# The global P V for both heads at once, dense pieces 0, 1, 2, 1 per step, and the local 1e-9 left on VectorE

## The chip, the core and the metric

The kernel runs on one core of a Trainium2 chip. The metric is the device time of one execution in microseconds; a program is compared by the median of several executions. The core has five engines with instruction streams of their own: TensorE (PE; its weight loads are listed as PEld), VectorE (DVE), ScalarE (ACT), GpSimd (POOL) and SyncE (SP, which issues most DMAs). They wait for each other by semaphores, and each engine runs its own stream in order.

## What is computed

Three layers follow each other. The first is attention with local and global tokens (batch 4, 8 heads, 512 local and 32 global tokens, head size 64, window 32); the second a dense layer of 512 → 2048 → 512 with PReLU on the 2176 tokens; the third sends each token to one of 8 experts. The change lies in the attention and in the part of the dense layer that runs beside it.

```python
def sm(s):
    s = s - np.max(s, axis=-1, keepdims=True)
    e = np.exp(s)
    return e / (np.sum(e, axis=-1, keepdims=True) + 1e-09)
s_g = scale * np.matmul(q_g, k_all.transpose(0, 1, 3, 2))      # 32 global rows see all 544 keys
out_g = np.matmul(sm(s_g), v_all)
s_ll = np.where(mask, scale * np.matmul(q_l, k_l.transpose(0, 1, 3, 2)), -1000000000.0)
s_lg = scale * np.matmul(q_l, k_g.transpose(0, 1, 3, 2))       # 512 local rows: window + 32 global keys
out_l = np.matmul(sm(np.concatenate([s_lg, s_ll], axis=-1)), np.concatenate([v_g, v_l], axis=2))
...
h = x @ w_in                                                   # the dense layer
g = np.maximum(h, 0.0) + alpha * np.minimum(h, 0.0)
x = g @ w_out
```

## The kernel before

**Units, pairs, steps.** A unit is one batch and two heads; there are 16 units, handled in 8 pairs p. A pair takes four steps j = 0 to 3 of 128 local positions (STEPS = 4), so that n = 4p + j runs from 0 to 31, with two more steps to drain. The order on TensorE, VectorE and ScalarE in the attention is the order of the program text (manual_schedule); on GpSimd and SyncE a scheduler sets it.

**One step** (attention, L489 to L536) is in this order: dense.turn (ScalarE: neg, the ReLU part of a finished dense product); norm of step n − 1 (VectorE L404, L405, L407: add 1e-9, reciprocal, scale the probabilities); scores of step n (TensorE s L391; VectorE L397 adds the mask and takes the maximum; ScalarE L399 exponentials with their sum); dense.close (VectorE g L559, ScalarE's ghi and GpSimd's glo, the high and low part of g for an exact product); two decoding operations on VectorE (fill "V": L85, L88, L90, L92, which unpack the dense layer's weights); the bank o and dummy products on it (L520); dense.products (six matmuls, L571 for the first dense product, L585 for the second); one of the four pieces of the global rows; more decoding; pv of step n − 2 (TensorE o L424, ScalarE's copy L426); ptrans of step n − 1 (TensorE t L413, ScalarE's copy L415); and ScalarE's decoding operations.

**The global rows.** Their pieces run at j = 1, 2, 3 and at j = 0 of the next pair: gscores (TensorE L440, VectorE L441, ScalarE exponentials L445), gnorm (VectorE L449 to L453: 1e-9, reciprocal, scaled probabilities into gpat), gtrans (six transposes gt L463, copies L464), gpv (go L473, copied into xb by L475). gpat is a fixed tile with zeros where no window has its own positions; GW names six windows that together cover all positions.

**The dense layer beside it.** From step 12 (BEG) a first chunk of 272 tokens (CH) goes through eight blocks f of the first product, twelve matmuls each in two halves of six, and from step 28 through the second product, block by block, into two accumulators (h) of the same pool h1. rest() does what is left of the second product behind the attention, and the GEMM stage (gemm, L208) follows; it decodes the other half of the weights, one part every ten yields. xl L73 and xh L72 are the low and high part of the next chunk's tokens xb.

**Banks.** PSUM tiles o and go rotate over the same pools: a new tile waits until the reader of the one that had its bank is done.

Of the kernel before, what the change touches and what calls it, by code (L numbers as in the profile page):

```python
# [25 lines left out]
def tile_attention_moe_moe(ctx: ExitStack, tc: tile.TileContext, qkw, vw,  # L26
# [285 lines left out]
    with ExitStack() as at:  # L312
# [115 lines left out]
        GW = (1, 4, 7, 10, 13, NQ - 2)  # L428

        def gscores(p, part):  # L430
            d = G[p]
            if part == 0:
                d["s"] = (gp.tile([128, NG], F32, name="gsc"), gp.tile([128, 4], F32, name="gmx", bufs=2))
            sc, mx = d["s"]
            lo, hi = (0, S) if part == 0 else (S, NG)
            s = bank([128, hi - lo], f"gs{part}")
            for i in range(2):
                k = U[2 * p + i]["k"]
                x = k[:, WIN:2 * WIN] if part else k[:, 2 * WIN:KL - WIN].rearrange("p (m c) -> p m c", c=3 * WIN)[:, :, :2 * WIN]
                T.matmul(s[64 * i:64 * i + 64], U[2 * p + i]["g"], x, start=True, stop=True)  # L440
            V.tensor_tensor_reduce(out=sc[:, lo:hi], in0=s, in1=gzero.to_broadcast([128, hi - lo]), scale=-D ** -0.5,  # L441
                                   scalar=mx[:, 0:1] if part else BIG, op0=OP.add, op1=OP.min,
                                   accum_out=mx[:, part:part + 1])
            if part:
                A.activation(out=sc, in_=sc, func=AF.Exp, bias=mx[:, 1:2], scale=-1.0, accum_out=mx[:, 2:3])  # L445

        def gnorm(p):
            sc, mx = G[p]["s"]
            V.tensor_scalar(mx[:, 2:3], mx[:, 2:3], 1e-9, None, op0=OP.add)  # L449
            V.reciprocal(mx[:, 3:4], mx[:, 2:3])  # L450
            own = gpat[:, 2 * WIN:KL - WIN].rearrange("p (m c) -> p m c", c=3 * WIN)[:, :, :2 * WIN]
            V.tensor_scalar(own, sc[:, :S].rearrange("p (m c) -> p m c", c=2 * WIN), mx[:, 3:4], None, op0=OP.mult)
            V.tensor_scalar(gpat[:, 4 * WIN:5 * WIN], sc[:, S:], mx[:, 3:4], None, op0=OP.mult)  # L453

        def gtrans(p, part):
# [5 lines left out]
            for i in range(n):  # L461
                o = kpos(GW[4 * part + i])
                T.transpose(t[:, i], gpat[:, o:o + KW], ident)  # L463
            (V.tensor_copy if part else A.copy)(d["t"][:, 4 * part:4 * part + n], t)  # L464

        def gpv(p):
            d = G[p]
            o = bank([128, 2, SG], "go")
            for i in range(2):
                for n, w in enumerate(GW):  # L470
                    r = slice(96 if w == NQ - 2 else 0, 128)
# [14 lines left out]

        def pieces(p):
            return [(0.8, lambda: (gscores(p, 0), gscores(p, 1))), (0.0, lambda: gnorm(p)),
                    (0.6, lambda: (gtrans(p, 0), gtrans(p, 1))), (1.2, lambda: gpv(p))]  # L489

        def attention():
# [9 lines left out]
            for n in range(N + 2):  # L501
# [9 lines left out]
                if n < N:  # L511
                    scores(p, j)
                dense.close(n)
# [24 lines left out]
        class dense:  # L538
            ps, ys, g = None, [], None

            def turn(n):
                f = (n - BEG) // 2 - 1
                if 0 <= f < KH and (n - BEG) % 2 == 0:
                    dense.neg = gh_.tile([128, CH], F32, name="neg")
                    A.activation(out=dense.neg, in_=dense.ps, func=AF.Relu, scale=-1.0)

            def close(n):
# [8 lines left out]
                f = (n - BEG) // 2 - 1  # L556
                if 0 <= f < KH and (n - BEG) % 2 == 0:
                    g = gh_.tile([128, CH], F32, name="g")
                    epi[0] = V.scalar_tensor_tensor(g, dense.neg, al1[:, f:f + 1], dense.ps, op0=OP.mult, op1=OP.add)  # L559
                    split(dense.g[0][:, f], dense.g[1][:, f], g, lo_eng=P)  # L560

            def products(n):
                f, half = divmod(n - BEG, 2)
                if f < 0:
                    return
                if f < KH:
                    if not half:
                        dense.ps = pH.tile([128, CH], F32, name="h1", tag="h1")
                    for k in (0, 1) if not half else range(2, KD):
# [3 lines left out]
                    return  # L573
                f = n - BEG - 2 * KH
                if not f:
                    dense.ys = [pH.tile([128, CH], F32, name="h1", tag="h1") for _ in range(2)]
                for d in range(2):
                    for _ in dense.second(d, (f,)):
                        pass
                dense.done = f + 1  # L580
# [9 lines left out]
            def rest():  # L590
                dense.ys += [pY.tile([128, CH], F32, name="y", tag="y") for _ in range(2)]
                most = KH - 2
                for d, fs in ((2, range(most)), (3, range(most))) + tuple(
                        (d, range(dense.done if d < 2 else most, KH)) for d in range(KD)):
                    yield from dense.second(d, fs)
                    if fs[-1] == KH - 1:
                        xd = gx.tile([128, CH], F32, name="xd", bufs=2)
                        A.copy(xd, dense.ys[d])
                        nc.sync.dma_start(out=xpart[d, :, :CH], in_=xd)
# [44 lines left out]
        gpat = mk.tile([128, KL], F32, name="gpat")  # L644
# [857 lines left out]
```

## Time and profile before

| | before |
|---|---|
| median of 3 runs | 819.95 us (819.55 to 821.95) |
| the profiled execution | 818.03 us |
| its span in the trace | 816.3 us |
| mean granted TensorE clock | 0.992 |
| TensorE busy, share of the span | 782.0 us, 96% |
| VectorE busy | 457.5 us, 56% |
| ScalarE busy | 392.6 us, 48% |
| GpSimd busy | 355.8 us, 44% |

A busy time says how long an engine worked, not whether its work set the end. Three other views tell that: the busy time of all engines in one stretch, the list of what each engine waited for, and the chain of waits, which goes back from the last instruction, at each step to what released it. In a timeline the figure in brackets at a row's end is the idle time of the engine ahead of that row, and what ended it.

### The profile page before, as it was taken

The numbers are of one execution on the slowest core, as the hardware profiler recorded it, in microseconds if no ns is written. First come the engines' busy times: TensorE is split into PE (matmuls) and PEld (weight loads), VectorE is DVE, ScalarE is ACT, GpSimd is POOL, SyncE is SP. The second block draws the span as 40 slices with busy tenths as digits, with TensorE's granted clock in tenths as the row PEclk, the third lists the DMA queues.
The fourth block names the chain that finished last, engine by engine and source line by source line (L and its number), as shares of the span: only waits on it lengthen the run. The fifth ranks groups of instructions, "written<-read, shape, count | busy, mean of one in ns | idle before, by whom it ended". The sixth has DMA issues, their size and how long they took to land.

```text
span 816.3 us, 20877 instructions
## 1 busy us (share of the span) xinstructions
PE 782.0 (96%) x8298; PEld 728.1 (89%) x8298; DVE 457.5 (56%) x1587; ACT 392.6 (48%) x983; POOL 355.8 (44%) x308
## 2 busy tenths in 40 slices
PE   6989897998999999999999999999999999999996
PEld 4767776898999999999999999999999999989994
DVE  5889997445556531434343357777767778652210
ACT  5777876444445533333333434342455655444431
POOL 1122222033445343300000555663799988688611
PEclk9999997999999999999999999999999999999999
DMA  9988785153433122022221216424376666566510
GB/s 341 374 300 284 284 301 169 52 173 125 133 126 91 50 84 83 7 65 69 74 92 56 83 55 214 128 66 156 101 226 200 204 212 182 155 186 207 189 55 28
DMA packets 53851, 121.98 MB, mean 149 GB/s; under 512 B 4600, under 2 KB 26040, under 8 KB 51705
## 3 DMA queue, kind: packets, MB, share of 16 engines
q1 hardware_dynamic: 50825, 111.73, 42.1%
q0 software_dynamic: 2928, 8.92, 3.0%
q8 instruction: 65, 1.06, 0.5%
q14 instruction: 33, 0.27, 0.1%
HBM read 102.80 MB, written 17.83 MB: 148 GB/s over the span
## 4 chain that ended last, share of the span: by engine, by line
PE 77%; DVE 9%; issue 5%; DMA 5%; POOL 2%; ACT 2%; SPq 0%; POOLq 0%; DVEq 0%; ACTq 0%
PE h L200 21%; PE h L1258 10%; PE h L1122 10%; PE y L239 9%; PE h L1102 8%; PE o L424 3%; PE s L391 2%; PE go L473 2%; DMA raw<-in_moe_w_in_dram 2%; PE h L1335 2%; PE lp L282 2%; PE t L413 1%; DMA raw<-in_moe_w_dram 1%; PE pc L938 1%; DVE sc L397 1%
## 5 line engine op out<-in xcount | busy, mean ns | idle before, releaser
L73 POOL TENSOR_TENSOR m<-raw,m 128x1024 fp32r<-128x1024 f32 x64 | 152.2, 2398 | 15.8 <-ACT m L72 12.8
L200 PE MATMUL h<-xh,win 128*128 128x272 f32 x704 | 138.5, 291 | 2.1 <-ACT xd L245 2.1
L200 PEld LDWEIGHTS h<-xh,win 128*128 128x128 f32 x704 | 111.9, 188 | 4.6 <-ACT xd L245 2.3
L73 POOL TENSOR_TENSOR gr<-gb,gr 128x272 fp32r<-128x272 f32 x64 | 48.0, 776 | 149.3 <-ACT gr L72 148.9
L1102 PE MATMUL h<-xsh,m 128*128 128x272 f32 x512 | 103.3, 293 | 0.0
L200 PE MATMUL h<-xl,win 128*128 128x272 f32 x352 | 101.3, 288 | 0.0
L1258 PE MATMUL h<-gr,wout 128*128 128x272 f32 x672 | 95.1, 294 | 0.0
L73 POOL TENSOR_TENSOR glo<-g,ghi 128x272 fp32r<-128x272 f32 x64 | 54.5, 856 | 91.2 <-ACT ghi L72 79.8
L1122 PE MATMUL h<-hh,m 128*128 128x272 f32 x448 | 91.4, 295 | 0.0
L1258 PEld LDWEIGHTS h<-gr,wout 128*128 128x128 f32 x672 | 87.0, 189 | 0.4 <-ACT gr L72 0.4
L239 PE MATMUL y<-ghi,wout 128*128 128x272 f32 x448 | 86.9, 290 | 0.0
L72 ACT CAST m<-raw 128x1024 fp32r<-128x1024 f32 x64 | 66.0, 1049 | 39.6 <-DMA raw<-in_moe_w_dram 39.6
L205 ACT ACTIVATE neg<-h 128x272 f32<-128x272 f32 x120 | 47.6, 397 | 71.2 <-PE h L200 70.5
L1102 PEld LDWEIGHTS h<-xsh,m 128*128 128x128 f32 x512 | 81.7, 189 | 0.1
L1102 PE MATMUL h<-xsl,m 128*128 128x272 f32 x256 | 74.0, 292 | 0.0
L206 DVE SCALAR_TENSOR_TENSOR g<-neg,al,h 128x272 f32<-128x272 f32 x56 | 27.5, 496 | 82.9 <-ACT neg L205 70.4
L1122 PEld LDWEIGHTS h<-hh,m 128*128 128x128 f32 x448 | 71.4, 188 | 1.7 <-issue 1.7
L239 PEld LDWEIGHTS y<-ghi,wout 128*128 128x128 f32 x448 | 70.9, 188 | 0.8 <-issue 0.8
L200 PEld LDWEIGHTS h<-xl,win 128*128 128x128 f32 x352 | 66.4, 188 | 0.0
L1122 PE MATMUL h<-hl,m 128*128 128x272 f32 x224 | 65.8, 294 | 0.0
L239 PE MATMUL y<-glo,wout 128*128 128x272 f32 x224 | 64.6, 289 | 1.1 <-POOL glo L73 1.1
L206 DVE SCALAR_TENSOR_TENSOR gb<-neg,al,h 128x272 f32<-128x272 f32 x64 | 31.3, 496 | 59.0 <-ACT neg L205 59.0
(286 smaller groups left out, 1638.9 us busy)
## 6 DMA issues: line engine op xcount, KB each, us to landing
raw<-in_moe_w_dram SPq DMA_DIRECT2D x64, 512.0 KB, 3.9
vv<-in_v_dram SPq DMA_DIRECT2D x16, 1024.0 KB, 9.2
qk<-in_qk_dram SPq DMA_DIRECT2D x14, 720.0 KB, 9.8
raw<-in_moe_w_in_dram SPq DMA_DIRECT2D x16, 512.0 KB, 4.8
raw<-in_moe_w_out_dram SPq DMA_DIRECT2D x16, 512.0 KB, 4.4
xb<-xs SPq DMA_DIRECT2D x15, 544.0 KB, 3.9
xs<-xb SPq DMA_DIRECT2D x16, 272.0 KB, 7.8
xpart<-xd SPq DMA_DIRECT2D x32, 136.0 KB, 1.7
```

The lines of the kernel that those rows point to most:

```text
L72: a = A.copy(hi, src)
L73: return a, (lo_eng or V).tensor_tensor(lo, src, hi.bitcast(F32), op=OP.subtract)
L200: T.matmul(ps, wi[:, w, k, fs], x[:, k], start=i == 0, stop=i == 3 * KD - 1)
L205: A.activation(out=neg, in_=ps, func=AF.Relu, scale=-1.0)
L206: epi[0] = V.scalar_tensor_tensor(g, neg, al1[:, hf * KH + f:hf * KH + f + 1], ps, op0=OP.mult, op1=OP.add)
L239: T.matmul(ps, wo[:, w, f, ds_], x[:, f], start=f == 0 and i == 0, stop=f == KH - 1 and i == 2)
L282: T.matmul(lp[r:r + 32], w, x, start=n < 4, stop=n >= LT - 4)
L391: T.matmul(s[e][lane(2 * a + h, i), ii // 2], queries(u, i)[r], U[u]["k"][r, kpos(i):kpos(i) + KW], start=True, stop=True)
L424: T.matmul(o[c, a, WIN * ii:WIN * ii + WIN], U[2 * p + a]["v"][:, i, c], d["t", j][:, ii, lane(2 * a + h, i)], start=True, stop=True)
L1102: T.matmul(ps, d["w1"][:, w, kk, f * 128:(f + 1) * 128], x[:, kk], start=kk == 0 and i == 0, stop=kk == KD - 1 and i == 2)
L1122: T.matmul(ps, d["w2"][:, w, f, ms], x[:, f], start=i == 0, stop=i == 3 * K3 - 1)
L1258: T.matmul(ps[j], wo[:, w, f, ds_], x, start=f == 0 and a == 0, stop=f == KH - 1 and a == 2)
```

## The change

It has four parts.

The global product (gpv) handles both heads in one matmul: the weights are all 128 columns of vv and the data 64 columns of gt, so that go becomes 128 x 64 per unit and holds each head's values against both heads' probabilities. The half that is wanted is copied out by two VectorE copies (spread_), put into a list `later` that is worked off in the next step, directly behind the scores. For this the last window is a full one of 128 positions, read from a wider gpat (KL + KW columns) into which gnorm writes one more copy of 32 columns.

gnorm goes through the same list, so it runs directly behind the scores of step j = 2 in place of behind close and two decoding operations. Its 1e-9 is added by GpSimd (in gscores). The local norm's 1e-9 (L404) stays on VectorE.

The dummy products at j = 0 are left out (four each at steps 4 and 8).

The dense pieces come as 0, 1, 2, 1 for j = 0 to 3 in place of one per step, two per step in the last two; closings (turn, close) follow the piece that ends a block. The second product's accumulators are taken one after the other, d = 0 first, and rest() has 48 matmuls in place of 60 and starts with both finished accumulators' copies.

```diff
-        GW = (1, 4, 7, 10, 13, NQ - 2)
+        GW = ((1, kpos(1)), (4, kpos(4)), (7, kpos(7)), (10, kpos(10)), (13, kpos(13)), (NQ - 2, KL))
...
             if part:
                 A.activation(out=sc, in_=sc, func=AF.Exp, bias=mx[:, 1:2], scale=-1.0, accum_out=mx[:, 2:3])
+                P.tensor_scalar(mx[:, 2:3], mx[:, 2:3], 1e-9, None, op0=OP.add)
+                later.append(lambda: gnorm(p))
...
-            V.tensor_scalar(mx[:, 2:3], mx[:, 2:3], 1e-9, None, op0=OP.add)
...
+            V.tensor_scalar(gpat[:, KL + 3 * WIN:], sc[:, S - WIN:S], mx[:, 3:4], None, op0=OP.mult)
...
-                    for h, c in heads():
-                        T.matmul(o[c, i], U[2 * p + i]["v"][r, w, c], d["t"][r, n, 64 * i + h * SG:64 * i + (h + 1) * SG],
-                                 start=n == 0, stop=n == len(GW) - 1)
-            V.tensor_copy(d["x"][:, :, :SG], o)
+                for n, (w, _) in enumerate(GW):
+                    T.matmul(o[:, i], U[2 * p + i]["v"][:, w], d["t"][:, n, 64 * i:64 * i + 64],
+                             start=n == 0, stop=n == len(GW) - 1)
+
+            def spread_():
+                for h, c in heads():
+                    V.tensor_copy(d["x"][c, :, :SG], o[c, :, h * SG:(h + 1) * SG])
+            later.append(spread_)
...
                 if n < N:
                     scores(p, j)
+                while later:
+                    later.pop()()
                 dense.close(n)
...
-                    for _ in range((4, 0, 2, 2)[j] if n < BEG else 0):
+                    for _ in range((0, 0, 2, 2)[j] if n < BEG else 0):
...
+                for _ in range((0, 1, 2, 1)[n % STEPS] if n < STEPS * NU // 2 else 2):
+                    at, dense.at = dense.at, dense.at + 1
+                    if at >= 2 * KH:
+                        f, d = divmod(at - 2 * KH, 2)
...
+                        for _ in dense.second(d, (2 * f, 2 * f + 1)):
+                            pass
+                        continue
...
+                    if half:
+                        dense.over.append((f, dense.ps))
```

What this does to the engines' orders is shown at two places. The first is VectorE in step 10, behind the last of the four local scores (ISA rows of L397); gmx holds the sum of the global rows, mag is a piece of weights being decoded. Before:

```order
L397 ISA mx 128x1
L85 TENSOR_SCALAR mag<-mag 128x512
L88 TENSOR_SCALAR mag<-mag 128x512
L449 TENSOR_SCALAR gmx<-gmx 128x1
L450 RECIPROCAL gmx<-gmx 128x1
L452 TENSOR_SCALAR gpat<-gsc,gmx 128x8x64
L453 TENSOR_SCALAR gpat<-gsc,gmx 128x32
L404 TENSOR_SCALAR sm<-sm 128x4
```

And after:

```order
L397 ISA mx 128x1
L451 RECIPROCAL gmx<-gmx 128x1
L453 TENSOR_SCALAR gpat<-gsc,gmx 128x8x64
L454 TENSOR_SCALAR gpat<-gsc,gmx 128x32
L455 TENSOR_SCALAR gpat<-gsc,gmx 128x32
L85 TENSOR_SCALAR mag<-mag 128x512
L88 TENSOR_SCALAR mag<-mag 128x512
L404 TENSOR_SCALAR sm<-sm 128x4
```

The global normalisation has moved ahead of the decoding, lost its addition and gained a copy.

The second place is TensorE from the end of the scores of step 28, with the semaphores that a row waits for (named by the engine that raises them). Before:

```order
L391 MATMUL s<-qk 32x128 x11
L585 MATMUL h_2610<-ghi,wout 128x272
L585 MATMUL h_2610<-glo,wout 128x272
L585 MATMUL h_2610<-ghi,wout 128x272 [waits Pool_49]
L585 MATMUL h_2611<-ghi,wout 128x272 [waits DVE_49]
L585 MATMUL h_2611<-glo,wout 128x272
L585 MATMUL h_2611<-ghi,wout 128x272
L473 MATMUL go<-gt,vv 64x32 [waits PE_49,Activation_49]
L473 MATMUL go<-gt,vv 64x32 x23
L424 MATMUL o<-pt,vv 64x32 [waits Activation_49]
L424 MATMUL o<-pt,vv 64x32 x15
```

After, from the same place:

```order
L391 MATMUL s<-qk 32x128 x11
L473 MATMUL go<-gt,vv 128x64 [waits DVE_49,Activation_49]
L473 MATMUL go<-gt,vv 128x64 x11
L424 MATMUL o<-pt,vv 64x32 [waits Activation_49]
L424 MATMUL o<-pt,vv 64x32 x15
```

And after, in step 29, from the global scores on:

```order
L440 MATMUL gs_2630<-qk 64x512 x2
L440 MATMUL gs_2634<-qk 64x32 [waits Activation_49]
L440 MATMUL gs_2634<-qk 64x32
L424 MATMUL o<-pt,vv 64x32 [waits DVE_49,Activation_49]
L424 MATMUL o<-pt,vv 64x32 x15
```

The six matmuls of the second dense product have left step 28, with the wait for VectorE that stood in front of the fourth; in step 29 the tile o (L424), which before waited for ScalarE alone, now waits for VectorE too: its bank is go's, which the spread copies free. On VectorE these stand behind step 29's scores, as this row shows it there after the change (the four rows ahead of it are two of the scores):

```order
L397 ISA sc,mx<-s,mask 128x128
L397 ISA mx 128x1
L397 ISA sc,mx<-s,mask 128x128
L397 ISA mx 128x1
L478 COPY xb<-go 64x2x32 x2
L90 SCALAR_TENSOR_TENSOR mag<-raw,mag 128x512
```

Before, one copy (L475) stood ahead of the local normalisation of step 28, one normalisation and four scores earlier.

## Rows read from the trace of the kernel before

**Rows 1.** From the page: TensorE's busy time, share of the span, instructions.

```profile
PE 782.0 (96%) x8298; PEld 728.1 (89%) x8298; DVE 457.5 (56%) x1587; ACT 392.6 (48%) x983; POOL 355.8 (44%) x308
```

**Rows 2.** Busy us of each engine by stage (instructions), clock, DMA share, GB/s.

```profile
20.00:56.00 36.00, 31.68 (x712) 24.86 (x718) 29.28 (x121) 25.53 (x92) 5.16 (x4) 1.00 0.88 327
56.00:134.00 78.00, 68.43 (x1468) 54.46 (x1468) 73.66 (x283) 63.78 (x219) 23.05 (x20) 1.00 0.82 292
134.00:160.00 26.00, 26.00 (x453) 21.80 (x454) 13.81 (x52) 13.51 (x47) 2.03 (x2) 0.80 0.14 46
160.00:200.00 40.00, 37.89 (x299) 37.56 (x299) 17.53 (x27) 16.80 (x41) 12.60 (x13) 1.00 0.50 163
```

**Rows 3.** Chain of waits in step 4: start us, us, what stood on it.

```profile
20.97 1.09 PE o L520 x8
22.06 1.88 PE go L473 x48
```

**Rows 4.** Waits from 20 to 56 us: engine, line, for what; total, times, longest.

```profile
DVE mag L85 <- ACT mag L83: 2.1, 3, 0.9
...
PE gt L463 <- DVE gpat L453: 2.1, 2, 1.7
```

**Rows 5.** VectorE's timeline at steps 6 and 10: start us, us, instruction.

```profile
32.93 0.15 DVE L449 TENSOR_SCALAR gmx<-gmx 128x1 f32<-128x1 f32 x1
...
33.71 0.23 DVE L453 TENSOR_SCALAR gpat<-gsc,gmx 128x32 f32<-128x32 f32 x1
33.86 0.68 DVE L90 SCALAR_TENSOR_TENSOR mag<-raw,mag 128x512 int32<-128x512 int32 x1
...
52.08 1.32 DVE L453 TENSOR_SCALAR gpat<-gsc,gmx 128x32 f32<-128x32 f32 x1
```

**Rows 6.** VectorE's groups, 56 to 134 us: busy us, mean ns, idle us before.

```profile
L397 DVE CUSTOM_DVE_ANT_0 sc<-s,mask 128x128 f32<-128x128 f32 x68 | 15.6, 283 | 0.0
L407 DVE TENSOR_TENSOR pr<-pr,sm 128x512 f32<-128x512 f32 x17 | 15.0, 883 | 0.6
```

**Rows 7.** What VectorE waited for from 56 to 134 us.

```profile
DVE g L559 <- ACT neg L545: 1.4, 2, 1.2
```

**Rows 8.** Two groups of GpSimd's subtractions from the page.

```profile
L73 POOL TENSOR_TENSOR m<-raw,m 128x1024 fp32r<-128x1024 f32 x64 | 152.2, 2398 | 15.8 <-ACT m L72 12.8
L73 POOL TENSOR_TENSOR gr<-gb,gr 128x272 fp32r<-128x272 f32 x64 | 48.0, 776 | 149.3 <-ACT gr L72 148.9
```

**Rows 9.** TensorE's timeline, step 28: the idle time stands in brackets.

```profile
134.00 0.42 PE L585 MATMUL h<-ghi,wout 128*128 128x272 f32 x1 [3.42 <-DVE g L559]
```

**Rows 10.** Four us of step 29, columns as in rows 2.

```profile
136.00:140.00 4.00, 4.00 (x63) 3.73 (x62) 2.73 (x5) 1.85 (x9) 0.76 (x1) 0.50 0.27 64
```

**Rows 11.** Chain of waits, steps 28 to 33.

```profile
134.87 3.14 PE go L473 x48
...
141.94 1.66 PE h L585 x6
...
145.14 0.93 PE o L424 x32
...
150.44 0.95 PE h L585 x6
...
158.73 1.12 PE o L424 x32
```

**Rows 12.** Timeline of ScalarE and VectorE in step 28.

```profile
135.19 1.10 ACT L72 CAST xh<-xb 128x1088 fp32r<-128x1088 f32 x1 [1.64 <-DMA xb<-xs]
136.32 1.29 DVE L73 TENSOR_TENSOR xl<-xb,xh 128x1088 fp32r<-128x1088 f32 x1 [1.58 <-ACT xh L72]
...
138.19 0.43 DVE L404 TENSOR_SCALAR sm<-sm 128x4 f32<-128x4 f32 x1
...
138.87 0.69 DVE L407 TENSOR_TENSOR pr<-pr,sm 128x512 f32<-128x512 f32 x1
```

**Rows 13.** TensorE's timeline behind the attention.

```profile
197.00 0.39 PE L200 MATMUL h<-xh,win 128*128 128x272 f32 x1 [2.11 <-ACT xd L245]
```

More of the change, by code (lines that the diff above doesn't have):

```diff
@@ L485, in tile_attention_moe_moe @@
         done = [-1]
+        later = []
         def pieces(p):
-            return [(0.8, lambda: (gscores(p, 0), gscores(p, 1))), (0.0, lambda: gnorm(p)),
+            return [(0.8, lambda: (gscores(p, 0), gscores(p, 1))), (0.0, lambda: None),
                     (0.6, lambda: (gtrans(p, 0), gtrans(p, 1))), (1.2, lambda: gpv(p))]
@@ L538, in tile_attention_moe_moe @@
         class dense:
-            ps, ys, g = None, [], None
+            ps, ys, g, at, over = None, [], None, 0, []
             def turn(n):
[L542 to L545, printed above, removed]
+                dense.neg = []
+                for f, ps in dense.over:
+                    neg = gh_.tile([128, CH], F32, name="neg")
+                    A.activation(out=neg, in_=ps, func=AF.Relu, scale=-1.0)
+                    dense.neg.append((f, ps, neg))
+                dense.over = []
             def close(n):
@@ L555, in close @@
                     split(dense.x[0][:, k], dense.x[1][:, k], XB[0][:, k, :CH], lo_eng=P)
-                f = (n - BEG) // 2 - 1
-                if 0 <= f < KH and (n - BEG) % 2 == 0:
+                for f, ps, neg in dense.neg:
                     g = gh_.tile([128, CH], F32, name="g")
-                    epi[0] = V.scalar_tensor_tensor(g, dense.neg, al1[:, f:f + 1], dense.ps, op0=OP.mult, op1=OP.add)
+                    epi[0] = V.scalar_tensor_tensor(g, neg, al1[:, f:f + 1], ps, op0=OP.mult, op1=OP.add)
                     split(dense.g[0][:, f], dense.g[1][:, f], g, lo_eng=P)
             def products(n):
-                f, half = divmod(n - BEG, 2)
-                if f < 0:
+                if n < BEG:
                     return
-                if f < KH:
+                for _ in range((0, 1, 2, 1)[n % STEPS] if n < STEPS * NU // 2 else 2):
+                    at, dense.at = dense.at, dense.at + 1
+                    if at >= 2 * KH:
+                        f, d = divmod(at - 2 * KH, 2)
+                        if not f:
+                            dense.ys.append(pH.tile([128, CH], F32, name="h1", tag="h1"))
+                        for _ in dense.second(d, (2 * f, 2 * f + 1)):
+                            pass
+                        continue
+                    f, half = divmod(at, 2)
                     if not half:
                         dense.ps = pH.tile([128, CH], F32, name="h1", tag="h1")
-                    for k in (0, 1) if not half else range(2, KD):
+                    for k in range(2 * half, 2 * half + 2):
                         for i, (w, x) in enumerate(((0, 0), (0, 1), (1, 0))):
@@ L572, in products @@
                                      start=k == 0 and i == 0, stop=k == KD - 1 and i == 2)
[L573 to L580, printed above, removed]
+                    if half:
+                        dense.over.append((f, dense.ps))
             def second(d, fs):
@@ L590, in rest @@
             def rest():
[L591 to L599, printed above, removed]
+                for d in range(KD):
+                    if d >= 2:
+                        dense.ys.append(pY.tile([128, CH], F32, name="y", tag="y"))
+                        yield from dense.second(d, range(KH))
+                    xd = gx.tile([128, CH], F32, name="xd", bufs=2)
+                    A.copy(xd, dense.ys[d])
+                    nc.sync.dma_start(out=xpart[d, :, :CH], in_=xd)
         queue = []
@@ L643, in tile_attention_moe_moe @@
         P.memset(gzero, 0.0)
-        gpat = mk.tile([128, KL], F32, name="gpat")
+        gpat = mk.tile([128, KL + KW], F32, name="gpat")
         P.memset(gpat, 0.0)
```

6 lines of the change are left out of this document (2 added, 4 removed).

## The prediction

> **What bounds the kernel now.** I read the page first: TensorE is busy for 782.0 us, 96% of the span [rows 1]. That is an average over stages, so I asked next for busy times by stage. The change lies in the attention, which ends at about 160 us, and just behind it. From 20 to 56 us (steps n = 4 to 11) TensorE is busy for 31.68 of 36.00 and VectorE for 29.28: neither is full, each waits in turn. From 56 to 134 (steps 12 to 28) VectorE is busy for 73.66 of 78.00: it sets the pace, and TensorE with 68.43 has room. From 134 to 160 TensorE is full, but at a mean granted clock of 0.80, and from 160 to 200 it is busy for 37.89 of 40.00 [rows 2]. Then I read in each stage the chain of waits, the list of waits and the timelines, for what stands directly behind each edit. The sum is made against the profiled execution (818.03 us, of which the span is 816.3); that lies 1.92 below the median 819.95, and I carry the difference over to the median.
>
> **Part 1, steps 4 to 11: the dummies and the global normalisation.** The four dummy products at steps 4 and 8 go: 8 records, 1.09 us, on the chain both times, directly between products of TensorE [rows 3]. Gain 2 × 1.09 = 2.18.
>
> At steps 6 and 10 the global normalisation stands behind two decoding operations, and for the first of these VectorE is idle until ScalarE's mag is there, 0.9 each time (of 2.1 us in three waits). TensorE's global transposes wait in turn for the last copy of the normalisation: 2.1 us in two waits, the longer 1.7 [rows 4]. The normalisation takes 0.93 (32.93 to what follows it at 33.86); the second time its last copy took 1.32 in place of 0.23 [rows 5]. In the new order it stands directly behind the scores. It loses the addition of one column (0.15) and gains a copy of 32 columns (0.15, the spacing from 33.71 to 33.86), so it keeps its length and fits into the idle 0.9. Both waits of TensorE should go: 2.1. The spread copy, now two of 0.15, costs 0.1 here. Part 1: −2.2 − 2.1 + 0.1 = **−4.2**. Bounds: −2.1, if the time of the dummies only turns into waits for VectorE; −5.2, if another microsecond of TensorE's short idle times closes too (36.00 − 31.68 = 4.3 in all). The loads move earlier with it: the 16 DMA engines are at 0.88 of their time in this stage [rows 2], but in its list of waits none is for a DMA, and as the waits stand I take nothing for them.
>
> GpSimd's addition is not in the trace. The nearest rows are its subtractions of 1024 and of 272 columns, 2398 and 776 ns; the line through them leaves 0.19 us for one column and 1.29 for 512 [rows 8]. It starts when ScalarE's exponentials of the global scores end, and VectorE has to finish the four local scores meanwhile (4 × 0.28 [rows 6]); I take nothing for it. With a split of 512 columns ahead of it on GpSimd up to 1.3 would show as a wait of VectorE for gmx, with close and the decoding queued behind.
>
> **Part 2, steps 12 to 27, where VectorE is the bound.** Per pair of units VectorE loses the addition (0.15) and gains a gpat copy and a spread copy (0.15 each): for four pairs +0.6. The order of the dense pieces, 0, 1, 2, 1 for 1, 1, 1, 1, gives TensorE the same four pieces in four steps, and TensorE has room: no cost. But the closings leave the steps in which the normalisation stands: VectorE waited there 1.4 us in two waits for ScalarE's neg [rows 7]. Half of it may come back where closings are now: −0.7. VectorE is also slowed by GpSimd's splits: the local normalisation takes 883 ns in the mean here [rows 6] and 0.69 undisturbed [rows 12], so 17 of them lose 3.3 us, and which are hit changes with the order: half of that either way, ±1.6. Part 2: **−0.1**, bounds −2.4 (−1.4 − 1.6 + 0.6) and +2.2.
>
> The product go itself changes from 48 records in 1.88 us (39 ns each) to 24 with 128 columns of weights and 64 of data. No such record exists before. Bound from below: 24 at 39 ns, 0.94. From above: a dummy has full weights and 128 columns of data and takes 137 ns (8 in 1.09), so 24 take 3.29 [rows 3]. With twice the data and half the records I take twice the 39 ns, 24 × 78 = 1.88, unchanged; it is also near half of the dummy's 137, with half of its data.
>
> **Part 3, steps 28 to 33.** Before, the second product's accumulator needs a bank that VectorE's g frees, and TensorE stands for 3.42 us until 134.00 [rows 9]; behind it the granted clock is 0.50 (1.2 GHz) [rows 10]. There go took 3.14 in place of 1.88 and six h 1.66 in place of 0.95 [rows 3, 11]: at a ratio of 0.6, the 10 us from 134 to 144 lost 4.0. In the new order no dense piece stands at step 28, and that wait is gone.
>
> A new one takes its place. At step 29 the tile o reuses go's bank and so waits for the spread copies, which VectorE now does a step later: behind xl, the local normalisation and the scores of step 29. On the times of before (all of it shifts together): go can start at about 130.1 (134.00 − 3.42 less three h that are gone). It and what follows up to the next o, also six h and the global scores, stood from 134.87 to 145.14, 10.27 us [rows 11], or 6.2 at the full clock: TensorE is at o by 136.3. VectorE does xl only from 136.32, since ScalarE's xh waited for the load xb until 135.19; xl takes 1.29. The local normalisation follows at about 137.9 (its exponentials now stand behind xh), with 0.68 to L407 and 0.69 for that [rows 12]; then four scores of 0.28 and the two copies, 0.3: 140.7. TensorE stands for about 4.4 us. An idle 1.7 left the clock at 1.00 (mean from 20 to 56 [rows 2]), one of 3.42 was followed by 0.50: I expect it to fall again, for the same 4.0. From this o to the end of the last took 145.14 to 159.85 before, 14.7; three more pieces stand in that stretch now, 18 products of 0.127 (299 in 37.89 [rows 2]), 2.3. End: 140.7 + 14.7 + 2.3 + 4.0 = 161.7 for 159.85. Part 3: **+1.8**. Bounds: −2.2 without the fall (a rival, below), +3.0 if spread slips by another normalisation of 1.2.
>
> **Part 4, behind the attention.** Twelve products fewer are left (48 for 60), 0.127 each: −1.5. The decoding of the later weights comes two yields later. TensorE's one wait there, 2.11 at 197 us for ScalarE's copy xd [rows 13], may vanish, or grow as much as the twelve products gain; I take no change. Part 4: **−1.5**, bounds −3.6 and 0.
>
> Sum: −4.2 − 0.1 + 1.8 − 1.5 = −4.0, so 814.0 against 818.03, and **815.9** against the median. The bounds taken as independent errors (1.6, 2.3, 1.2 and 1.8) give ±3.6: 812.3 to 819.5.
>
> **Rivals.** (B) The clock stays at 1.00 at step 29, because spread comes earlier and the idle time stays nearer to 1.7 than to 3.4. For it: the clock took 1.7 without harm. Against it: xh, xl, normalisation and scores stand in one chain of VectorE. Another −4.0: 811.9.
>
> (C) In the old form the two heads' products ran side by side in the two column halves, and the new one costs the upper bound, 3.29. For it: 39 ns is little beside the dummy's 137. Against it: the dummy has twice the columns of data. +1.41 at the three places where TensorE sets the pace (steps 4, 8 and 32); in steps 12 to 27 TensorE's room hides it. 3 × 1.41 = 4.2: the gain is gone, 820.1, no change. The Trainium skill's page "TensorEngine Tiling (Array Packing)", section "Theoretical Speedup", speaks against the change in the same way: a dimension of at most 64 gains up to twofold by tiling, which the new form gives up. By its full factor go would take 3.76 and the sum would come to 821.5; the trace of before has no row for it.
>
> (D) Slower: without the dummies TensorE stands longer in steps 4 to 11, and its clock falls there. The 2.18 are then waits, and one fall costs what the one behind 134 us did, 4.0: −2.1 + 4.0 − 0.1 + 1.8 − 1.5 = +2.1, 822.1; two falls, 826.1. It decides as soon as one idle time lies well above 1.7, towards 3.42. Against it: each place loses only 1.09 of work, and the gap of 1.7 is one of those that the moved normalisation closes.
>
> (E) The change doesn't take the work off VectorE, as GpSimd's addition is stuck behind a split: half of 1.29 at four pairs, +2.6: 818.5.
>
> **How the numbers follow.** Chances: forecast 0.54, B 0.20, C 0.13, D 0.07, E 0.06. A measurement tells 0.3% from no change, 2.5 us: faster is below 817.5, slower above 822.4. Of the forecast some 72% lie below 817.5 (0.39); with B whole, and a fifth of C and a third of E, faster has 0.64. Slower is half of D and a third of C with their spread, 0.08; same the rest, 0.28. The range goes from 810.5, a little under B, to 820.2, which takes in C's 820.1; left out are the lower edge of B, the upper half of C, and D.
>
> **What the profile after would show.** Part 1: no L520 at steps 4 and 8, global transposes that don't wait for gpat, a stage 4 us shorter. Part 2: the same step time, a mean of L407 near 883, no wait of VectorE for GpSimd. go: 24 records in about 1.9 us; near 3.3 is C. Part 3: no wait of h for g; a wait of o for the spread copy (xb, VectorE) at step 29 of about 4.4 us with a lower clock behind it; a clock of 1.00 there is B, one under 1.00 ahead of step 28 is D. The prediction is wrong if go is slow, or if the time behind the attention changes by more than the twelve products.

## The result, and the profile after

The changed kernel takes 826.84 us (median of 9 executions, 824.45 to 833.36), the kernel before 819.99 in the same comparison: ratio 1.011, 95% interval 1.0087 to 1.0133. The change is slower by 1.1%, where 815.9 and a gain of 4 us were forecast; the range ended at 820.2. The profiled execution took 826.68 us, its span 824.9, its mean granted clock 0.980 (before: 0.992). One execution of e14 below, 1221.98 us at a mean clock of 0.558, is in a slow state and left out of every figure.

Busy time of each engine by stage of the changed kernel, to be read against [rows 2]; the clock is the third number from the end:

```profile
20.00:56.00 36.00, 32.97 (x600) 26.44 (x599) 27.67 (x113) 23.83 (x84) 5.19 (x6) 0.86 0.79 299
56.00:134.00 78.00, 73.49 (x1317) 60.89 (x1324) 69.20 (x267) 58.72 (x206) 21.49 (x22) 0.91 0.78 280
134.00:160.00 26.00, 20.96 (x373) 17.20 (x354) 19.87 (x78) 17.05 (x58) 6.02 (x6) 0.87 0.38 118
160.00:200.00 40.00, 40.00 (x391) 39.55 (x390) 19.50 (x31) 17.18 (x42) 12.04 (x12) 1.00 0.42 136
```

Two things stand out. The clock, at 1.00 up to 134 us before, is below it in the first two stages. And TensorE is busy for longer with fewer instructions: 32.97 us with 600 matmul records from 20 to 56, before 31.68 with 712.

TensorE's timeline in the changed kernel shows both in go (start us, us, instruction; in brackets the idle time ahead and what ended it), at steps 4, 8, 12, 20 and 24:

```profile
20.49 2.89 PE L473 MATMUL go<-gt,vv 128*128 128x64 f32 x24
...
37.69 4.97 PE L473 MATMUL go<-gt,vv 128*128 128x64 f32 x24 [1.10 <-ACT gt L466]
...
60.33 3.84 PE L473 MATMUL go<-gt,vv 128*128 128x64 f32 x24 [1.39 <-ACT gt L466]
...
100.42 3.04 PE L473 MATMUL go<-gt,vv 128*128 128x64 f32 x24 [1.23 <-ACT gt L466]
...
120.67 2.86 PE L473 MATMUL go<-gt,vv 128*128 128x64 f32 x24 [0.20 <-ACT xb L426]
```

At a full clock go takes 2.8 us, not 1.9. And at three of the steps it now waits 1.1 to 1.4 us for ScalarE's copy of the global transposes; there the clock falls while go runs. Four microseconds each, columns as above:

```profile
36.00:40.00 4.00, 2.90 (x45) 2.63 (x45) 3.37 (x16) 4.00 (x15) 1.02 (x1) 0.77 1.00 402
40.00:44.00 4.00, 4.00 (x39) 3.88 (x40) 2.00 (x5) 1.01 (x6) 0.25 (x1) 0.50 0.76 309
44.00:48.00 4.00, 4.00 (x50) 2.28 (x50) 1.32 (x11) 1.93 (x7) 0.00 (x0) 0.50 0.01 2
```

VectorE, busy for 3.4 of 4 us ahead of the fall, has 1.32 of 4 to do at its end: everything waits for TensorE at half speed.

### The profile page after: what moved, and what is told of

Its sections match the earlier page's. It is cut to its first block, busy times and chain, and to the rows that moved or that the text cites. A ratio compares the mean times of both kernels' runs of the same rounds, so it can differ in the third digit from the quotient of the medians.

```text
span 824.9 us, 20480 instructions
## 1 busy us (share of the span) xinstructions
PE 793.7 (96%) x8090; PEld 740.3 (90%) x8090; DVE 460.2 (56%) x1595; ACT 392.7 (48%) x983; POOL 359.4 (44%) x316
## 4 chain that ended last, share of the span: by engine, by line
PE 75%; DVE 8%; DMA 5%; POOL 5%; issue 4%; ACT 2%; SPq 0%; POOLq 0%; DVEq 0%; ACTq 0%
PE h L200 21%; PE h L1267 10%; PE y L239 9%; PE h L1111 8%; PE h L1131 8%; PE go L473 2%; PE o L424 2%; POOL m L73 2%; DMA raw<-in_moe_w_dram 2%; PE h L1344 2%; PE lp L282 1%; PE t L413 1%; PE s L391 1%; DVE sc L397 1%; DMA xs<-xb 1%
```

## The experiments

The theories after this look: **cover** (the dummies and the dense piece at j = 0 stood in front of go and covered its wait for gt; without them TensorE stands, and its clock falls) and **length** (the new go is longer, and that is the loss). A third, that GpSimd's addition holds VectorE up, is tried last. All ratios are to the kernel before on the same chip; its medians beside these runs went from 818.61 to 821.25 us, so medians of two rows compare only to some 2.6 us, and the ratios decide. "Clock" is the range of the mean granted clocks of the runs.

| run | change on what | median us | ratio (95%) | clock |
|---|---|---|---|---|
| changed kernel | | 826.84 | 1.011 (1.0087 to 1.0133) | 0.972 to 0.985 |
| e1 | changed, dummies of steps 4, 8 back | 825.38 | 1.0049 (1.0021 to 1.0076) | 0.983 to 0.993 |
| e2 | changed, one dense piece per step | 820.87 | 0.9995 (0.9969 to 1.0022) | 0.987 to 0.995 |
| e3 | changed, dummies at every j = 0 | 819.97 | 0.9982 (0.9962 to 1.0002) | 0.993 to 0.997 |
| e4 | changed, old go | 814.93 | 0.9927 (0.9897 to 0.9956) | 0.980 to 0.994 |
| e5 | before, moved normalisation alone | 818.41 | 0.9978 (0.9957 to 1.0000) | 0.983 to 0.990 |
| e6 | before, new go alone | 828.70 | 1.0114 (1.0082 to 1.0146) | 0.979 to 0.991 |
| e7 | e4 with e1 and e2 | 818.45 | 0.9974 (0.9946 to 1.0001) | 0.982 to 0.994 |
| e8 | e4, early transposes | 815.60 | 0.9930 (0.9898 to 0.9961) | 0.985 to 0.999 |
| e9 | e4, xl moved | 816.25 | 0.9974 (0.9949 to 1.0000) | 0.976 to 0.991 |
| e10 | e4 with e2 | 819.63 | 1.0019 (0.9997 to 1.0041) | 0.981 to 0.991 |
| e12 | before, go lengthened | 829.75 | 1.0123 (1.0089 to 1.0157) | 0.976 to 0.989 |
| e13 | e4 with e3 | 817.18 | 0.9967 (0.9940 to 0.9994) | 0.987 to 0.997 |
| e14 | e4, split in step 31 | 813.55 | 0.9938 (0.9906 to 0.9971) | 0.981 to 0.993 |
| e15 | e13 and e14 | 809.15 | 0.9883 (0.9834 to 0.9932) | 0.999 |
| e16 | changed, global 1e-9 on VectorE | 827.78 | 1.0117 (1.0050 to 1.0185) | 0.975 to 0.984 |
| e17 | e15 with the new go | 815.33 | 0.9942 (0.9920 to 0.9964) | 0.997 to 0.999 |
| e18 | e7 and e14 | 813.00 | 0.9899 (0.9848 to 0.9951) | 0.990 to 0.997 |

### Cover put back

e1 puts the dummies of steps 4 and 8 back, on the changed kernel:

```diff
-                    for _ in range((0, 0, 2, 2)[j] if n < BEG else 0):
+                    for _ in range((4, 0, 2, 2)[j] if n < BEG else 0):
```

> The changed kernel (826.8 us) with the four dummy products at j = 0 of steps 4 and 8 put back. Cover theory: in the changed kernel TensorE waits 1.10 us for ScalarE's copy gt in front of go at step 8, and its clock falls to 0.5 there; the steps 8 to 11 took 22.1 us where before they took 19.4. With the dummies the wait is covered, the clock stays at 1.00 up to step 12, these steps take about 19, and the time is about 824. Length theory (the new go takes 2.82 us in place of 1.88, and that is the loss): the dummies cost their 2 x 1.09 on top, 828 to 829.

e2 has one dense piece per step in place of 0, 1, 2, 1, on the changed kernel:

```diff
-                for _ in range((0, 1, 2, 1)[n % STEPS] if n < STEPS * NU // 2 else 2):
+                for _ in range(1 if n < STEPS * NU // 2 else 2):
```

> The changed kernel with one dense piece in every step from 12 to 31 in place of 0, 1, 2, 1, all else as changed. Cover theory: a piece of about 0.95 us stands in front of go again at steps 12, 16, 20, 24, so the waits of 1.39 and 1.23 us for gt at steps 12 and 20 are covered, the two falls of the clock there go, each worth about 3.3 us (periods of 21.5 us and more against 18.3): 819 to 821, with the fall at step 8 left. Length theory: TensorE's work from 12 to 28 is the same, so no change: 826 to 827.

e3 has dummies at every j = 0 from step 4 to 28, on the changed kernel:

```diff
-                    for _ in range((0, 0, 2, 2)[j] if n < BEG else 0):
+                    for _ in range((4, 0, 2, 2)[j] if n < BEG else 4 if j == 0 and n < N else 0):
```

> The changed kernel with four dummy products in front of go at every j = 0 from step 4 to 28, dense pieces 0, 1, 2, 1 as changed. Cover theory: no fall of the clock ahead of step 28, since something always stands in the gap in front of go; all periods about 18.3 us, 817 to 820, although TensorE has 7 x 1.09 us more to do. Length theory: 7.6 us more work on the engine that loses time, 830 to 834.

All three came out on the side of cover. e1 is not slower for its 2.2 us of dummies, e2 gains 6 us with the same work, and e3, with 7.6 us more work on TensorE, gains 7. In e3's profile the clock is below 1.00, up to 200 us, only between 140 and 146, behind the wait at step 29; go takes 2.8 to 2.9 at each step and waits for nothing. The wait for gt isn't gone, it stands in front of the dummies now, 0.46 to 0.92 us at four of the steps, and the clock stays up; step 12 as an example:

```profile
56.86 1.16 PE L528 MATMUL o<-ident 128*128 128x128 f32 x8 [0.92 <-DVE gt L466]
57.86 2.79 PE L473 MATMUL go<-gt,vv 128*128 128x64 f32 x24
```

So the fall of the clock cost more than the work that prevents it.

### The length of go

e4 has the old go with its copy, on the changed kernel:

```diff
-                for n, (w, _) in enumerate(GW):
-                    T.matmul(o[:, i], U[2 * p + i]["v"][:, w], d["t"][:, n, 64 * i:64 * i + 64],
-                             start=n == 0, stop=n == len(GW) - 1)
...
+                for n, (w, _) in enumerate(GW):
+                    r = slice(96 if w == NQ - 2 else 0, 128)
+                    for h, c in heads():
+                        T.matmul(o[c, i], U[2 * p + i]["v"][r, w, c], d["t"][r, n, 64 * i + h * SG:64 * i + (h + 1) * SG],
+                                 start=n == 0, stop=n == len(GW) - 1)
+            V.tensor_copy(d["x"][:, :, :SG], o)
```

> The changed kernel with the old global P V: 48 records with 64 columns of weights per pair, one copy directly behind. Length theory: go is back at 1.88 us, 8 x 0.94 = 7.5 us less, about 819, and the clock stays up. Cover theory: the wait for gt in front of go remains, the clock still falls at steps 8, 12 or 20; only where TensorE sets the pace 0.9 each is gained, and the wait at step 29 for the spread copy goes (the copy stands at step 28 again): 822 to 825.

e6 is the kernel before with these lines the other way, with spread_ and the wider gpat.

> The kernel before with the new global P V alone (24 records with 128 columns of weights, spread copies in the next step); dummies, dense pieces and normalisation as before. Length theory: go takes 2.8 in place of 1.9 us; it is paid where TensorE sets the pace (steps 4, 8, 32) and perhaps in the middle steps: 823 to 827. Cover theory: dummies and dense pieces still stand in front of go, so the clock doesn't fall ahead of step 28, and the cost is no more than the 3 x 0.94 plus the new wait for spread at step 29, which adds to the wait of 3.4 us at step 28: 823 to 826. Under both it is slower; a granted clock below 1.00 ahead of step 28 would speak against the cover theory.

e11 is e3 with half the data in go (one execution, read for its trace alone):

```diff
-                    T.matmul(o[:, i], U[2 * p + i]["v"][:, w], d["t"][:, n, 64 * i:64 * i + 64],
+                    T.matmul(o[:, i, :32], U[2 * p + i]["v"][:, w], d["t"][:, n, 64 * i:64 * i + 32],
...
-                    V.tensor_copy(d["x"][c, :, :SG], o[c, :, h * SG:(h + 1) * SG])
+                    V.tensor_copy(d["x"][c, :, :SG], o[c, :, :SG])
```

> The changed kernel with four dummies at every j = 0, and in go only 32 of the 64 columns of data, so that half of the global rows are left out of the result: what a record costs by its data and what by its weights. If the 116 ns of a record follow the data (the prediction's view: 39 ns for 32 columns, twice that for 64), 24 records take about 1.4 us. If they follow the load of 128 columns of weights, they take about 2.7 as with 64.

e12 is the kernel before with four products without use right behind go, whose tile is widened for them:

```diff
+            for _ in range(4):
+                T.matmul(o[:, :, SG:], ident, ident[:, :2 * SG].rearrange("p (i c) -> p i c", i=2), start=True, stop=True)
```

> The kernel before with four dummy products of 128 x 128 weights and 64 columns right behind go, 0.9 us more of TensorE work at each of the eight steps j = 0, and nothing else. The new P V alone (same 0.93 us, spread copies, wider pattern) gave 8.6 us more than before. If the length of go is that whole loss, also in the steps in which VectorE is busy for 94%, this gives 7 to 9 us more, 827 to 829. If TensorE's room hides it in the steps 12 to 27, as the prediction had it, it is 3 x 0.9 more, 823.

The length counts too, and more than either theory said. e4 lies 12 us below the changed kernel, lower than both expectations; e6, with all cover in place, is 8.6 us slower than before by go (with its copies) alone, above both expectations too. e11 says why go is longer; its timeline of TensorE at step 4:

```profile
20.62 2.76 PE L473 MATMUL go<-gt,vv 128*128 128x32 f32 x24
```

Half the data, the same time: in both kernels a record starts 112 ns behind the one before. In e12 the records with the same width of weights and 64 columns of data start 112 ns apart as well, behind a go of the old form:

```profile
20.80 1.95 PE L473 MATMUL go<-gt,vv 128*64 128x32 f32 x48
22.68 1.10 PE L476 MATMUL go<-ident 128*128 128x64 f32 x8
```

And so do the dummies of the kernel before, with 128 columns of data: their 137 ns is a mean that holds the longer gaps ahead of the second record and behind the last (213 and 205 ns). So between 32 and 128 columns the data don't set the price here; what these records share is 128 columns of weights.

The old go runs otherwise. In the trace of the kernel before its records start in pairs, 7 ns apart within a pair, mostly 58 ns from one pair to the next: two records with 64 columns of weights pass in about half the time of one with 128. The mean of 39 ns is higher than 29 because of three gaps of some 150 ns, where the windows change from 128 rows to 32 and back. This is what rival C described, products that run side by side, as far as the trace tells: it doesn't say whether the two of a pair belong to the two heads. Half as many records at 112 ns make go 1.5 times as long.

And e12 shows that TensorE's room in the middle steps doesn't hide it: 1.0 us more at each of eight steps cost 11 us against the kernel before on the same chip (818.61), some 4 of them the clock's at the price worked out below. The busy times of e6 from one go (step 12) to another (step 28), columns as in [rows 2]:

```profile
58.86:139.73 80.87, 71.44 (x1337) 58.35 (x1337) 74.72 (x287) 62.10 (x213) 22.49 (x20) 1.00 0.77 273
```

The same of the kernel before:

```profile
57.45:134.80 77.35, 67.78 (x1434) 53.91 (x1433) 72.98 (x280) 62.33 (x215) 22.58 (x20) 1.00 0.81 287
```

In e6 the stretch is 3.5 us longer, 1.7 of it more busy time of VectorE, its extra copies among it (74.72 against 72.98), and 1.8 VectorE's idle time (6.15 against 4.37). An engine that is busy for 94% of a stretch still waits in the step in which the other one gets longer.

### The parts that gain

e5 is the kernel before with the normalisation moved and its addition on GpSimd:

```diff
-            V.tensor_scalar(mx[:, 2:3], mx[:, 2:3], 1e-9, None, op0=OP.add)
...
+                P.tensor_scalar(mx[:, 2:3], mx[:, 2:3], 1e-9, None, op0=OP.add)
+                later.append(lambda: gnorm(p))
...
+                while later:
+                    later.pop()()
```

> The kernel before with one part of the change alone: the global normalisation directly behind the scores of step j = 2, its 1e-9 on GpSimd. If the gain that the prediction saw there is real (TensorE's waits of 0.45 and 1.69 us for gpat at steps 7 and 11 go), this is 817 to 819 against 820 to 821, with the clock at 1.00 up to step 28. If GpSimd's addition gets stuck behind its splits, VectorE waits for it and the time is 821 or more.

e7 is e4 with the lines of e1 and e2, e10 is e4 with that of e2.

> The changed kernel with the old global P V, the dummies of steps 4 and 8 back, and one dense piece in each step from 12 to 31: what is left of the change is the moved normalisation and the second dense product with one accumulator after the other. If length and cover together are the whole loss, the time lies below both kernels, 809 to 813, with no clock below 1.00 ahead of step 28. If something else of the change costs (GpSimd's addition, the order of the second dense product), it stays at 815 or above.

> The changed kernel with the old global P V and one dense piece per step, without dummies at j = 0. It is the fourth corner of a square: new P V with 0, 1, 2, 1 gave 826.8, new with one per step 820.9, old with 0, 1, 2, 1 814.9. If the lengths of go and the cover of its wait add up, 814.9 - 5.9 = 809. If the cover matters only together with the long go, which comes into the slow clock behind the wait, it stays near 814 to 816.

e16 is the changed kernel with the global addition back on VectorE: the two lines of e5 with 1e-9, the other way.

> The changed kernel (826.8) with the global rows' 1e-9 back on VectorE, directly in front of the reciprocal, all else as changed. If GpSimd's addition has no part in the loss: 826 to 828 (8 x 0.15 us more on VectorE at most). If VectorE waited for GpSimd, 823 to 825.

The moved normalisation alone gains 0.2% (e5), in the range expected, though its interval touches no change. Its clock, expected at 1.00 up to step 28, fell twice earlier, at 38 us behind a wait of 1.93 us in the scores and at 93 us behind one of 1.33 for pr: with all cover in front of go. e16 clears GpSimd's addition: with it back on VectorE the time is the same. e7 and e10 are misses: with the old go, one dense piece per step is slower than 0, 1, 2, 1 (ratios 0.9974 and 1.0019 against 0.9927 for e4), the other way round than with the new go.

In e10's profile the clock falls at five places, at two of them behind a go that waited for nothing. But TensorE stood elsewhere there, in o right behind go and in the next scores, for nothing that the profile shows ("issue"):

```profile
98.09 0.64 PE L424 MATMUL o<-pt,vv 128*64 128x32 f32 x8 [1.52 <-issue]
120.67 1.18 PE L391 MATMUL s<-qk 64*32 64x128 f32 x25 [1.82 <-issue]
```

From 20 to 165 us TensorE's waits for gt in front of go are 3.6 us in e4 and 1.2 in e10; those for pt and pr, in other parts of the steps, are 2.1 and 5.4. So cover in front of go can move the waiting instead of ending it, and go is not the only place where a wait is followed by a fall.

### The wait for go taken away, and the gap at step 29

e8 is e4 with the first global transposes ahead of the local exponentials, in scores:

```diff
+            if j == 3:
+                gtrans(p, 0)
...
-                    (0.6, lambda: (gtrans(p, 0), gtrans(p, 1))), (1.2, lambda: gpv(p))]
+                    (0.6, lambda: gtrans(p, 1)), (1.2, lambda: gpv(p))]
```

> The changed kernel with the old global P V and with the first four global transposes and ScalarE's copy of them ahead of the local exponentials of step j = 3; dummies and dense pieces 0, 1, 2, 1 as changed. This takes away what go waits for, in place of covering it. If the wait for ScalarE's gt is what lets the clock fall, the falls at steps 8, 12 and 20 go and the time is 809 to 813. If the clock falls all the same (because the steps j = 0 hold too little work for TensorE), it stays near 815, with other waits in front of go or behind it.

e9 is e4 with the split issued after the last local normalisation:

```diff
-        splitx(1, 0)
+        with tc.issue_after(last[0].ins):
+            splitx(1, 0)
```

> The changed kernel with the old global P V, and with the split of the second chunk's tokens (xh on ScalarE, xl on VectorE), which stands in step 28 and waits there for a load, moved behind the last local normalisation. In the changed kernel ScalarE and VectorE are idle for 4.4 us in front of that split and TensorE for 5.0 in two waits. If this load is what opens the gap at steps 28 and 29, the gap and the fall of the clock behind it go: 5 to 7 us less than the 814.9 of the run with the old P V alone, 808 to 811. If the gap comes from VectorE's chain of normalisation and scores instead, it stays, 813 to 815.

e14 is e4 with the split in the loop over the attention's steps:

```diff
+                if n == STEPS * NU // 2 - 1:
+                    splitx(1, 0)
...
-        splitx(1, 0)
```

> The changed kernel with the old global P V and the second chunk's split written out in step 31, so that ScalarE's xh too leaves step 28 (in the run with the late split only VectorE's xl had left it, and ScalarE still waited there for the load). Clock theory: no gap and no fall of the clock at steps 28 to 31; 3 us of waiting and 4 us of low clock go: 808 to 812. If the gap comes from elsewhere (VectorE's chain), 814 to 816.

e13 is e4 with the line of e3, e15 is e13 with the split of e14, e17 is e15 with the new go, and e18 is e7 with the split of e14.

> The changed kernel with the old global P V and four dummy products in front of go at every j = 0 from step 4 to 28. Clock theory: without the falls at steps 8, 12 and 20 (some 10 us at half clock in the profile of the run without these dummies) the time is below 814.9 although 7 x 1.09 us of work are added, 809 to 813. If the work on TensorE decides, it is above, 818 to 822.

> Both together: old global P V, four dummies at every j = 0, split in step 31. Clock theory: clock at 1.00 through the whole attention, 805 to 810. If the two gains overlap, or the dummies cost what they take, 812 to 816.

> The changed kernel with four dummies at every j = 0 from step 4 to 28 and the second chunk's split in step 31; the new global P V stays. Against the same kernel with the old one (809.15), if the clock stays up: 8 x 0.93 = 7.4 us more, 816 to 817, if TensorE's length counts in full; 812 if it counts only at steps 4, 8 and 32.

> The changed kernel with the old global P V, one dense piece per step in place of 0, 1, 2, 1, dummies only at steps 4 and 8, and the split in step 31. If cover is what keeps the clock, useful work serves as well: clock at 0.995 or more, and 5 x 1.09 us of dummies less, 805 to 809. If the clock falls all the same at some places, 812 to 818.

e8 took the wait for ScalarE's gt away and gained nothing: TensorE's timeline at step 8 has two other waits in its place, and the clock falls again (0.64 from 40 to 44 us).

```profile
35.90 0.27 PE L477 MATMUL go<-gt,vv 128*64 128x32 f32 x2 [0.49 <-DVE gt L468]
36.95 1.94 PE L477 MATMUL go<-gt,vv 128*64 128x32 f32 x46 [0.78 <-issue]
```

TensorE runs ahead of VectorE there, and whatever it meets next holds it. e9 didn't test what it was meant to: xl left step 28, but ScalarE's xh stayed there and waited 3.54 us for the load. e14 moved both. Alone it shows no clear gain (813.55 against 814.93, but a ratio of 0.9938 against 0.9927, with clocks between 0.981 and 0.993). e13 alone is not faster either (0.9967), above the range that the clock theory gave; its clock fell at step 8, behind a wait of 1.52 us in the scores ahead of the dummies, and at step 29. Both together (e15) keep the clock at 1.00 in all four stages, and give the fastest kernel of this study:

```profile
20.00:56.00 36.00, 32.49 (x735) 25.19 (x733) 30.17 (x121) 25.52 (x92) 5.94 (x6) 1.00 0.86 320
56.00:134.00 78.00, 75.13 (x1594) 62.40 (x1594) 74.73 (x289) 66.03 (x228) 25.73 (x25) 1.00 0.82 295
134.00:160.00 26.00, 26.00 (x409) 23.56 (x408) 11.28 (x47) 13.06 (x42) 1.65 (x2) 1.00 0.41 130
160.00:200.00 40.00, 38.91 (x310) 38.69 (x309) 25.82 (x40) 21.50 (x50) 20.30 (x21) 1.00 0.38 121
```

809.15 us, 1.2% below the kernel before, and its four executions lie within 2.2 us (808.25 to 810.46), where the other kernels spread by 4 to 11. e17, the same with the new go, takes 815.33, also at a full clock: **the new go alone costs 5 to 6 us**, 6.2 by the medians and 4.8 by the two ratios, where eight times 0.93 would be 7.4. In e18 useful work covers as well as dummies at most places (0.990 to 0.997), but the clock still falls at 91 us, behind a wait of 1.35 for pr, and it is not faster than e15.

### How much the clock costs

The runs of one kernel differ in their clock, which gives its price. Over 156 executions of the kernels in the table, each measured from its own kernel's mean, a microsecond of granted clock lost ((1 − clock) × time) goes with 0.73 us of time (correlation 0.86). This is a correlation: a wait that lengthens a run and lets its clock fall counts in it too. For the changed kernel the loss is 16.5 us (1 − 0.980, of 826.84), 12.1 us of time at this price; for the kernel before, in its five sets of runs, 8.9 to 11.0 us, or 6.5 to 8.0 of time. Taken off, 814.8 and 811.8 to 813.2 are left: by this estimate the clock makes up 4 to 6 of the 7 us that the change costs, and 2 to 3 remain. With the new go alone (e6) 821.0 are left, with e4 807.8. The sum behind the result is then, as an estimate: some 7 us lost by go (5 to 6 by e17 against e15), some 5 gained by the other parts, and 4 to 6 lost by the clock.

## Why the prediction was wrong, step by step

**Part 1, −4.2 forecast.** The mechanism was right and the outcome wrong. The normalisation does fit into VectorE's idle time, and TensorE's transposes no longer wait for gpat. TensorE's waits from 20 to 56 us after the change (engine, line, for what; total, times, longest):

```profile
PE o L424 <- ACT pt L415: 1.3, 2, 0.8
PE go L473 <- ACT gt L466: 1.1, 1, 1.1
PE o L424 <- DVE xb L478: 0.4, 1, 0.4
```

But step 12 begins 2.1 us later than before, not 4.2 earlier. The step that failed is the dummies' gain: the 2.18 for the dummies came in part at step 4 (steps 4 to 7 take 16.02 us for 16.21, although go is 0.9 longer), while at step 8 the 1.09 us came back as a wait of 1.10, the lower bound that the text named, and behind it the clock fell: steps 8 to 11 take 22.1 us for 19.4. Starts of step 12 and step 28 on TensorE, after:

```profile
58.04 0.90 PE L391 MATMUL s<-qk 64*32 64x128 f32 x32
...
137.52 0.67 PE L391 MATMUL s<-qk 64*32 64x128 f32 x32
```

**Part 2, −0.1 forecast.** From step 12 to step 28 the changed kernel takes 79.5 us, before 73.2 (55.90 to 129.10): +6.3. Two steps failed. "TensorE has room: no cost" counted the pieces of four steps together; in the step j = 0 itself nothing was left that covered go's wait (1.39 and 1.23), and a longer go is not hidden there either (e6: 3.5 us more at a full clock, its copies included). And go was taken at 1.88 us: of the two ways to scale, by the data columns (39 ns doubled) and by the width of the weights (a dummy's), the prediction chose the first, and e11 shows that the data don't count. The upper bound, 3.29, held the measured 2.8; its 137 ns was a mean over eight records, which start 112 ns apart like the new go's.

Rival C had the mechanism: the single records of the old go, two in 58 ns, stood in the trace of before, and the text says that it has no row for it. Its 3.76, by the full factor, was not reached, since the old form also has the three gaps of 150 ns. And C put the cost at three steps; by e6 the middle ones pay too. The Trainium skill's page "TensorE: Matmul & The Clock Gate", section "LDWEIGHTS (loading the stationary operand)", says that a load's time goes in proportion to the columns of the weights, whatever the rows. The trace is near it, 112 ns for 128 columns and 58 for 64, but two records share the 58.

**Rival D** had the right mechanism, a fall of the clock for want of dummies, and the wrong point from which it decides: it asked for an idle time well above 1.7 us, because one of 1.7 had done no harm before. After the change a fall followed one of 1.10. It had also looked at steps 4 to 11 alone, while the dense pieces' leaving j = 0 did the same at steps 12 and 20.

**Part 3, +1.8 forecast, +1.9 measured.** Step 28 begins 8.4 us late and the last o ends 10.3 late (170.17 against 159.85). The new wait is there, about as long as forecast (4.4), in two pieces: TensorE stands 3.04 us in front of the last global scores, for ScalarE, which has xh's wait for the load ahead of it, and 2.00 in front of o, for spread; the clock is 0.50 behind it. Timeline of TensorE and ScalarE:

```profile
145.22 1.10 ACT L72 CAST xh<-xb 128x1088 fp32r<-128x1088 f32 x1 [4.38 <-DMA xb<-xs]
...
148.50 0.43 PE L440 MATMUL gs<-qk 128*64 128x32 f32 x4 [3.04 <-ACT xb L426]
150.93 1.92 PE L424 MATMUL o<-pt,vv 128*64 128x32 f32 x32 [2.00 <-DVE xb L478]
```

The agreement is partly luck: go's extra 0.9 at steps 28 and 32 was not in the sum.

**Part 4, −1.5 forecast.** The lateness shrinks from 10.3 us at the attention's end to 8.0 where the router's first logits stand (370.6 against 362.6): −2.3, the twelve products and a part of TensorE's one wait, which is 0.56 instead of [rows 13]. At the end of the span it is 8.6; the last 0.6 were not traced.

**GpSimd's addition** takes 0.21 us, where the line through two subtractions had given 0.19, and holds nobody up (e16). **E** is out.

What stays open: what exactly makes the clock fall. It fell behind waits from 0.71 us (e10, step 8) to 1.93 (e5), but not behind 1.69 in the kernel before, 1.18 in e15, or 1.23 in e1, whose wait for gt at step 20 is as long as the one that a fall follows in the changed kernel. Open too is why one dense piece per step is slower than 0, 1, 2, 1 once go is short: the clock doesn't tell it (mean 0.987 in e10, 0.988 in e4).

## What to carry to other kernels

Price a new matmul from the row with the same width of weights, not from the row with the nearest data: here a record cost 112 ns with 32, 64 and 128 columns of data alike, and two narrow ones passed in 58. Look at the starts of single records before a group's time is divided by its count. Before work is moved away from a place, ask what the engine would wait for without it; filler that only covers a wait can be worth more than it takes, since the slowed clock charges everything behind it. And cover on average is none: look at the step in which the wait stands.

## What was not expected of the hardware

Little decides whether the clock falls: 7.6 us of products with no result (e3) saved 7 us against the same kernel without them. The kernel with a clock of 0.999 (e15) is also the one whose time repeats best, within 0.3% over four executions; e17, at 0.997 to 0.999, stays within 0.6% over ten, and those at 0.97 to 0.99 spread by about 1%. Much of the spread of this kernel's time goes with its clock.
